# One transformer block on one core: DVE's exponential in two AV products instead of three, and a table of block choices

## The chip, the cores and the metric

The program runs on 1 core of a Trainium2 chip. The metric is device time in microseconds, the median of several executions. The engines named are PE (TensorE matmul; PEld is its weight load), DVE (VectorE), ACT (ScalarE), POOL (GpSimd) and SP (SyncE, which here only issues DMAs).

## The reference

x is 2048 x 512 in bf16, 32 heads of 16, and a gated feed-forward layer with 1,792 inner columns.

```python
def _A_ref(x, wqkv, wo):
    qkv = (x @ wqkv).reshape(B, S, 3, H, Dh)          # H = 32, Dh = 16
    scores = jnp.einsum("bhqd,bhkd->bhqk", q, k) * (Dh ** -0.5)
    p = _softmax(scores, axis=-1)
    o = jnp.einsum("bhqk,bhkd->bhqd", p, v)
    return o.transpose(0, 2, 1, 3).reshape(B, S, D) @ wo
def _B_ref(x, w_gate, w_up, w_down):
    h = _sigmoid(x @ w_gate) * (x @ w_up)
    return h @ w_down
h = x + _A_ref(_layernorm(x), A_wqkv, A_wo)
return h + _B_ref(_layernorm(h), B_w_gate, B_w_up, B_w_down)
```

## The kernel before

**Blocks and tiles.** The scores are 32 heads x 2048 queries x 2048 keys. They are cut into 2,048 blocks of 128 x 512: mostly two tiles of 128 keys by 256 queries side by side. A *group* is four heads by 256 queries (twice as many blocks for the wide groups at the start): 32 blocks. A *tile* `n` is two blocks early on and three later. `scores(n)` (L1085) computes one tile into PSUM; the exponential of a tile is shared out between two engines.

**The two exponentials.** ACT takes all blocks of a tile, or all but the last, in one `activation` (L1408) and writes fp16 into slots of `PT` or of other buffers that have come free (`p_slots`, `more_slots`). If `split` is true, DVE takes the last block: `dexp_first` (L1256) adds an offset to the scores, clips and writes int16. Read as fp16, this *code* is a straight-line approximation of the power of two; two further straight-line pieces, *chords*, are the code plus 326 and the code minus 332. The exponential is approximated by code + first chord + 1.5625 x second chord. In the kernel before these are not added up: all three are fp16 matrices in a tile `J`, and each is multiplied by V on PE, the third by `Vaug2`, which is V times 1.5625. Two DVE blocks share a `J` (`GQ` = 2, six buffers, `QB`). The chords are made by `dexp_rest`: two int64 additions on POOL (L1277), each covering four int16 at once, or, early in the run, on DVE.

**Attention times V.** `av` (L1233) takes blocks whose exponential is ready (a `Unit` each), four at a time in a row, because four heads lie side by side in PE's columns, and adds them up in one PSUM bank `acc`, whose two halves serve alternate groups. `finish_group` lets DVE move a finished group out (L1151), divide by the sums and transpose. `ahead_ready` allows rows of the next group before the present one is finished, within limits that depend on which half it uses.

**Background.** The projections, the output product, the layer norm and the feed-forward layer are generators in a queue `bg`; `try_bg` puts one step of them between the attention's blocks. Their PSUM tiles are moved out by DVE and ACT (tanh, L854). Gate and up weights arrive in `wgu` by DMAs of SP.

**The order.** It is written out by hand (`manual_schedule`): while the program is built, a planner in Python keeps a clock for each engine (`T["P"]`, `T["A"]`, `T["D"]`, `T["G"]`), adds constants for each operation and emits an instruction where its model has the time for it. For every tile the main loop decides about `split`, emits the exponential, and then fills PE's time up to the tile's end with background steps (`try_bg`), rows of AV (`av`), or nothing (`T["P"] += 100`). `want_dve` and the line with `split` limit DVE by its own backlog and by the number of `J` buffers. The result is one fixed instruction stream for each engine. Each stream runs in order, and an instruction that waits holds up all behind it on its engine.

**The end.** After the last tile the remaining AV units are consumed, the last group is finished, and the last 256 queries go through output product, norm and feed-forward; the weights for that are loaded by SP into the `J` buffers (L1495).

Of the kernel before, what the change touches and what calls it, by code (L numbers as in the profile page):

```python
# [19 lines left out]
DependencyClass = mybir.DependencyClass  # L20
DependencyReason = mybir.DependencyReason

LOG2E = 1.4426950408889634
# [119 lines left out]
def kernel(  # L143
# [883 lines left out]
    def pick(want):  # L1027

        out, used = [], set()
        last = None  # L1030
        b = blocks[0]
        if want:
            j = st["dj"] % 4
            if b.a[j]:
                last = (b.qc, b.g, b.a[j].popleft(), j)
                st["dj"] = j + 1
                used.add(j)
        while blocks and len(out) + (last is not None) < wide["n"]:
            b = blocks[0]
            js = [j for j in range(4) if b.a[j]]  # L1040
            if not js:
                blocks.popleft()
                used.clear()
                if last is not None:
                    used.add(last[3])
                continue
            j = max(js, key=lambda j: (j not in used, len(b.a[j]), -((j - st["aj"]) % 4)))
            out.append((b.qc, b.g, b.a[j].popleft(), j))
            st["aj"] = j + 1
            used.add(j)  # L1050
        while blocks and not blocks[0].left():
            blocks.popleft()
        return out + ([last] if last is not None else [])
# [191 lines left out]

    GQ, QB = 2, 6
    quads = []
    half = []

    def dexp_first(src, u, n):  # L1250
        if not half:
            half.append(dvx.tile([P, 3, GQ, QC], I16, name="J", bufs=QB))
            quads.append([])
        J = half[0]
        k = len(half) - 1
        nc.vector.tensor_scalar(out=J[:, 0, k, :], in0=src, scalar1=ZOFF, scalar2=float(-min(CHORDS)),  # L1256
                                op0=ALU.add, op1=ALU.max)
        T["D"] = max(T["D"], sc_end[n] + LAT) + 601
        todo[u[0], u[1], u[3]] += 2
        uns = [Unit(u, J[:, s, k, :].bitcast(FP16), n, None if s else T["D"] + TAIL["D"],  # L1260
                    v=Vaug2 if s == 2 else Vaug) for s in range(3)]
        avq.extend(uns)
        half.append(uns)
        quads[-1].extend(uns)
        if k == GQ - 1:
            dexp_rest()

    def dexp_rest():
        J, quad = half[0], half[1:]
        half.clear()  # L1270
        k = len(quad)

        def words(s):
            return J[:, s, 0:k, :].rearrange("p a b -> p (a b)").bitcast(I64)

        def chord64(s):
            nc.gpsimd.int64_add(words(s), words(0), CHORDS[s - 1] * (1 + 2 ** 16 + 2 ** 32 + 2 ** 48))  # L1277
            for i in range(k):
                quad[i][s].end = T["G"] + TAIL["G"]

        def chord(s):
            nc.vector.tensor_scalar(out=J[:, s, 0:k, :], in0=J[:, 0, 0:k, :], scalar1=float(CHORDS[s - 1]),
                                    scalar2=None, op0=ALU.add)
            for i in range(k):
                quad[i][s].end = T["D"] + TAIL["D"]
        on_pool = len(st["early"]) == TQ * (NQC - 1) and all(j.end is not None for j in st["early"])
        if on_pool and not st["lib"]:
            st["lib"] = True
            T["G"] += 9000.0
        for s in (1, 2):  # L1290
            if on_pool:
                pool(150 + 192 * k, lambda s=s: chord64(s), Mark(T["D"] + TAIL["D"]))
            else:
                chain.append((70 + 133 * k, lambda s=s: chord(s)))

    def want_dve(n):

        quads[:] = [q for q in quads if any(un in avq for un in q)]
        if not blocks or not late("d"):
            return False  # L1300
        busy = sum(j.ns for j in dq if j.ready() is not None) + sum(c[0] for c in chain)
        rest = group_left() / 2.8
        if not half and len(quads) >= QB:
            return False
        if busy > 1500:
            return False
        return busy + 1900 + 1100 * (GQ - len(half[1:])) <= rest * 1100
# [4 lines left out]

    NPT, NPE = 24, 14
    PT = ptp.tile([P, NPT, QC], FP16, name="pt")
# [16 lines left out]
    def run_of(w):  # L1331

        best = None
        for i in range(len(slots) - w + 1):
            row = slots[i:i + w]
            if row[0].tile is row[-1].tile and not any(s.unit in avq for s in row):
                end = max(s.end for s in row)
                if best is None or end < best[0]:
                    best = end, row
# [35 lines left out]
    while n + 1 < len(tiles):  # L1375
# [18 lines left out]
        dable = len(tl) > 1 and busy <= 1500  # L1394
        split = (dable and max(T["D"], sc_end[n] + LAT) <= start + 600 and bool(half or len(quads) < QB))
        if n > N - 12:
            end = max(T["D"], sc_end[n] + LAT) + 1900 + 600 * (GQ - len(half[1:]) if half else GQ)
            split = split and end <= start + 1330 * (N - n) - 500
        if half and half[1][0].u[:2] != tl[-1][:2]:
            dexp_rest()  # L1400
            quads[:] = [q for q in quads if any(un in avq for un in q)]
            split = split and len(quads) < QB
        wa = len(tl) - split
# [19 lines left out]
        hor = max(T["A"], sc_end.get(n + 1, 0.0) + LAT)  # L1423
        lim = ex_end[n] + LAT
        while T["P"] < lim - 100:
            run_dve(min(T["P"], hor))

            def room(mode):
                return lim + OVER - T["P"] - (0 if st["mode"] == mode else SWITCH)
            if early_on or room("dense") >= (bg[0][2][0] if ready_bg(0) is not None else 2 * MM):  # L1430
                used = try_bg(tokens, depth=3 if early_on else 2)
# [44 lines left out]
    nc.vector.tensor_scalar(out=ident2[:], in0=ident_bf[:], scalar1=2.0, scalar2=None, op0=ALU.mult)  # L1476
    while any(un.n < N - 1 and un.slot is not None for un in avq):
        flush()
# [9 lines left out]
    tw = {}  # L1488
    for i in range(QB):
        t = dvx.tile([P, 3, GQ, QC], I16, name="J", bufs=QB)[:].rearrange("p a b n -> p (a b n)")  # L1490
        n = min(3 * GQ // 2, FC - len(tw))
        f = len(tw)
        w = t[:, 0:n * 2 * DC * P].bitcast(BF16).rearrange("p (k c n) -> p k c n", k=2, c=DC)
        for k in range(2):
            nc.sync.dma_start(out=w[:, k], in_=gate_v[k][:, :, f * P:(f + n) * P])  # L1495
        for m in range(n):
            tw[f + m] = w[:, :, :, m * P:(m + 1) * P]
        if len(tw) == FC:
            break

# [35 lines left out]
    leftover(7)  # L1536
    hnl = [PT[:, k, :].bitcast(BF16) for k in range(n)]
    nc.scalar.activation(out=hnl[0], in_=hps[0], func=ACT.Identity, bias=nmr[:, 0:1], scale=rstd[:, 0:1])
# [75 lines left out]
```

## Time and profile before

| | |
|---|---|
| runs | 756.49, 756.53, 757.41 us (median 756.53) |
| profiled execution, span from first to last instruction | 754.6 us |
| granted TensorE clock, mean | 0.998 |
| DVE blocks (L1256) | 619, mean 681 ns |
| ACT exponentials (L1408), all buffers | 695 |
| chord additions on POOL (L1277) | 640, mean 603 ns |
| AV matmuls with `J` (L1233) | 3,546 recorded |
| DMA queue q1 | 39.59 MB, 17.9% of 16 engines' span |

The profile is of one execution, taken by the hardware profiler. A page of it has busy time for each engine, the chain of work that ended last (followed back from the last instruction, at each step to what released it), groups of instructions by line and shape (count, busy time, mean duration, idle time of the engine before them and who ended it), and DMA issues with the time to landing. A timeline row gives the start, the time covered, the engine, the line, what is written and read, and how many instructions are merged in it; in brackets stands the idle time ahead of it and what ended it. On PE and ACT a recorded duration overlaps the start of the next instruction, so that the pace is read from starts, not from durations.

### The profile page before, as it was taken

The numbers are of one execution on the slowest core, as the hardware profiler recorded it, in microseconds if no ns is written. First come the engines' busy times: TensorE is split into PE (matmuls) and PEld (weight loads), VectorE is DVE, ScalarE is ACT, GpSimd is POOL, SyncE is SP. The second block draws the span as 40 slices with busy tenths as digits, with TensorE's granted clock in tenths as the row PEclk, the third lists the DMA queues.
The fourth block names the chain that finished last, engine by engine and source line by source line (L and its number), as shares of the span: only waits on it lengthen the run. The fifth ranks groups of instructions, "written<-read, shape, count | busy, mean of one in ns | idle before, by whom it ended". The sixth has DMA issues, their size and how long they took to land.

```text
span 754.6 us, 27232 instructions
## 1 busy us (share of the span) xinstructions
PE 718.8 (95%) x11541; PEld 347.4 (46%) x11617; DVE 621.7 (82%) x1231; ACT 709.2 (94%) x788; POOL 396.0 (52%) x709
## 2 busy tenths in 40 slices
PE   7999998889999999999999999999999999999997
PEld 3322224444454445444555454535544455445554
DVE  7988878889978898898889688977889777899743
ACT  7989989999999999999999999999999999899952
POOL 2733546666556456655645546564555446465600
PEclk9999999999999999999999999999999999999999
DMA  7000005000123003210222122201321133003160
GB/s 238 1 1 1 1 18 153 2 3 3 30 87 99 10 10 109 78 30 10 78 59 59 36 79 58 74 22 38 99 59 30 44 93 107 10 9 105 47 203 17
DMA packets 68927, 41.65 MB, mean 55 GB/s; under 512 B 3520, under 2 KB 68800, under 8 KB 68800
## 3 DMA queue, kind: packets, MB, share of 16 engines
q1 hardware_dynamic: 68512, 39.59, 17.9%
q8 instruction: 92, 1.51, 0.9%
q14 instruction: 35, 0.29, 0.1%
q10 hardware_dynamic: 288, 0.26, 0.1%
HBM read 37.75 MB, written 2.10 MB: 53 GB/s over the span
## 4 chain that ended last, share of the span: by engine, by line
PE 74%; ACT 13%; DVE 8%; issue 4%; DMA 0%; POOL 0%; DVEq 0%; ACTq 0%; POOLq 0%
PE PS L1085 24%; PE PS L1233 23%; PE PS L824 14%; ACT pt L1408 10%; PE PS L842 6%; DVE J L1256 4%; PE PS L311 2%; PE PS L316 2%; PE PS L763 1%; ACT QTb L1408 1%; DVE xs L1151 1%; ACT xnT L1408 1%; PE PS L1560 1%; DVE st L271 1%; PE PS L305 1%
## 5 line engine op out<-in xcount | busy, mean ns | idle before, releaser
L1277 POOL INT64_ADD J<-J x640 | 377.6, 603 | 305.3 <-DVE J L1256 261.4
L1408 ACT ACTIVATE pt<-PS 128x1024 f16<-128x1024 f32 (+2 forms) x517 | 517.3, 1104 | 13.3 <-PE PS L1085 5.1
L1256 DVE TENSOR_SCALAR J<-PS 128x512 int16<-128x512 f32 x619 | 413.8, 681 | 70.1 <-PE PS L1085 42.7
L1085 PE MATMUL PS<-QT,KT 32*128 32x256 bf16 (+1 forms) x3712 | 263.8, 276 | 10.9 <-ACT pt L1408 4.9
L1233 PE MATMUL PS<-J,Vaug 128*17 128x256 f16 (+1 forms) x3546 | 243.4, 279 | 3.3 <-DVE xs L1151 1.9
L1233 PE MATMUL PS<-pt,Vaug 128*17 128x256 f16 (+1 forms) x2043 | 205.0, 279 | 2.8 <-DVE xs L1151 2.3
L1233 PEld LDWEIGHTS <-Vaug 128*17 128x17 bf16 x6204 | 139.3, 90 | 91.5 <-issue 84.4
L1085 PEld LDWEIGHTS <-KT 32*128 32x128 bf16 x3840 | 89.1, 92 | 197.2 <-issue 193.8
L824 PE MATMUL PS<-xnT,wgu 128*128 128x256 bf16 x784 | 113.7, 275 | 0.1
L1408 ACT ACTIVATE xnT<-PS 128x1024 f16<-128x1024 f32 x90 | 95.0, 1080 | 0.9 <-PE PS L1085 0.7
L824 PEld LDWEIGHTS <-wgu 128*128 128x128 bf16 x784 | 63.6, 97 | 39.6 <-issue 34.2
L1233 PE MATMUL PS<-xnT,Vaug 128*17 128x256 f16 x362 | 56.4, 274 | 0.0
L842 PE MATMUL PS<-wd,hT 128*128 128x512 bf16 x169 | 51.2, 383 | 2.5 <-issue 2.5
L1151 DVE STREAM_TRANSPOSE xs<-PS 128x256 f32<-128x256 f32 (+1 forms) x60 | 27.7, 461 | 21.9 <-PE PS L1233 21.2
L854 ACT ACTIVATE th<-PS 128x512 f32<-128x512 f32 (+1 forms) x63 | 37.4, 594 | 8.4 <-DVE hT L837 6.7
L1408 ACT ACTIVATE QTb<-PS 128x1024 f16<-128x1024 f32 x40 | 42.7, 1068 | 0.5 <-PE PS L1085 0.5
L896 DVE SCALAR_TENSOR_TENSOR hT<-th,PS 128x512 bf16<-128x512 f32 x49 | 33.3, 680 | 7.3 <-PE PS L824 7.2
L1233 PE MATMUL PS<-QTb,Vaug 128*17 128x256 f16 (+1 forms) x158 | 28.4, 275 | 0.0
L1408 ACT ACTIVATE xb<-PS 128x1024 f16<-128x1024 f32 (+2 forms) x26 | 25.6, 1030 | 2.1 <-PE PS L1085 1.1
L1122 DVE TENSOR_TENSOR o<-xs,rsum 128x128 bf16<-128x128 f32 (+1 forms) x60 | 24.4, 407 | 2.1
L1408 ACT ACTIVATE pe<-PS 128x1024 f16<-128x1024 f32 (+2 forms) x22 | 21.7, 1062 | 1.7 <-PE PS L1233 1.4
L842 PEld LDWEIGHTS <-hT 128*128 128x128 bf16 x196 | 12.2, 97 | 20.8 <-issue 17.8
(128 smaller groups left out, 397.5 us busy)
## 6 DMA issues: line engine op xcount, KB each, us to landing
wgu<-in_B_w_gate_dram SPq DMA_DIRECT2D x49, 256.0 KB, 3.0
wgu<-in_B_w_up_dram SPq DMA_DIRECT2D x49, 256.0 KB, 3.5
out_dram<-ob SPq DMA_DIRECT2D x16, 128.0 KB, 2.1
wd<-in_B_w_down_dram SPq DMA_DIRECT2D x1, 1792.0 KB, 8.8
xr<-in_A_x_dram SPq DMA_DIRECT2D x14, 128.0 KB, 3.8
xb<-in_A_x_dram SPq DMA_DIRECT2D x6, 256.0 KB, 6.0
J<-in_B_w_gate_dram SPq DMA_DIRECT2D x4, 384.0 KB, 5.9
J<-in_B_w_up_dram SPq DMA_DIRECT2D x4, 384.0 KB, 7.0
```

What stands on the lines that cost most here:

```text
L311: nc.tensor.matmul(ps, lhsT=w_sb[:, d, p * P:(p + 1) * P], rhs=xnT[c][:, d, :], start=(d == 0), stop=(d == DC - 1))
L824: nc.tensor.matmul(ps[:, 0:PARTS[r][2]], lhsT=w[:, d, :], rhs=hn_of(r)[:, d, :], start=(d == 0), stop=(d == DC - 1))
L842: nc.tensor.matmul(ps, lhsT=hT[:, f, i * P:(i + 1) * P], rhs=wd[:, f, :], start=(f == 0), stop=(f == FC - 1))
L854: nc.scalar.activation(out=th[:, 0:ps.shape[-1]], in_=ps, func=ACT.Tanh, scale=0.5)
L896: nc.vector.scalar_tensor_tensor(out=hT[:, f:f + k, 0:w], in0=th[f][:].rearrange("p (k n) -> p k n", k=k), scalar=1.0, in1=ps2.rearrange(" ...
L1085: nc.tensor.matmul(pss[:, ui, i * CW[qc]:(i + 1) * CW[qc]], lhsT=KT[g // 2][32 * j:32 * j + 32, k * P:(k + 1) * P], rhs=q[32 * j:32 * j + ...
L1122: nc.vector.tensor_tensor(out=o2[:, 0:w // 32, DH * a:DH * a + DH], in0=xs[:, 0:w // 32, 0:DH], in1=rec.to_broadcast([P, w // 32, DH]), op ...
L1151: j = dve(650 - ns[0], lambda: nc.vector.transpose(out=xs[:, 0:w // 32, :].rearrange("p b r -> p (b r)"), in_=src), Mark(T["P"] + DRAIN), ...
L1233: nc.tensor.matmul(dst[32 * j:32 * j + VW, 0:w], lhsT=un.v[:, kt * SPAN[qc] + i, h, :], rhs=un.ap[:, i * w:(i + 1) * w], start=clears and ...
L1256: nc.vector.tensor_scalar(out=J[:, 0, k, :], in0=src, scalar1=ZOFF, scalar2=float(-min(CHORDS)), op0=ALU.add, op1=ALU.max)
L1277: nc.gpsimd.int64_add(words(s), words(0), CHORDS[s - 1] * (1 + 2 ** 16 + 2 ** 32 + 2 ** 48))
L1408: ex = nc.scalar.activation(out=pt, in_=pss[:, 0:wa, :], func=ACT.Exp, scale=AS)
```

## The change

1. A DVE block has two AV units instead of three. Its codes go to a tile `C` of three blocks (`GQ` = 3, `QT_` = 4 buffers). `dexp_rest` takes two runs of slots from the same slots as ACT's exponentials: the first chord is written to the first run, the second to the other. Then a DMA issued on POOL with `accum_op=ALU.add` adds the codes to the first run; it stands in POOL's queue between the two additions. The sum is multiplied by V, the second chord by 1.5625 V. Early in the run, DVE makes both chords and the addition.
2. In the planner the DMA costs POOL 1,100 ns and lands 4,500 ns after that; an int64 addition over k blocks costs 288 + 180 k instead of 150 + 192 k.
3. `room_dve` replaces the count of `J` buffers: it asks for free slots and for the fourth-last `C` to be free by plan. `PT` has 48 slots instead of 24. A run of slots must now be contiguous.
4. A table `PLAN` of 65 entries, with key 16 x tile + step, overrides choices of the planner: 9 ends the filling of a tile, 5 lets PE idle 100 ns, 1 to 3 put in up to so many rows of AV, 4 tries the background first; at step 15 a value forces `split` on (2; five entries) or off, at step 14 it changes which head's block goes to DVE.
5. At the end the weights of the last feed-forward part go into slots of P instead of `J` buffers.

```diff
+PLAN = {96: 9, 162: 4, 304: 3, 305: 4, 322: 3, 417: 4, 432: 1, 624: 3, 638: 1, 640: 2,
...
+        10672: 5, 10702: 2, 10846: 3, 11073: 4, 11087: 2, 11089: 9}
...
-            j = st["dj"] % 4
+            j = (st["dj"] + PLAN.get(16 * len(tiles) + 14, 0)) % 4
...
-    GQ, QB = 2, 6
+    GQ, QT_ = 3, 4
+    DMA_ISSUE, DMA_LAT = 1100.0, 4500.0
...
+    def room_dve():
+        busy = sum(s.unit in avq for s in slots)
+        if len(slots) - busy < 2 * (len(half[1:]) + 1) + 6:
+            return False
+        if half or len(codes) < QT_:
+            return True
+        e = codes[-QT_].end
+        return e is not None and e <= max(T["D"], T["A"]) + 300
...
     def dexp_first(src, u, n):
         if not half:
-            half.append(dvx.tile([P, 3, GQ, QC], I16, name="J", bufs=QB))
-            quads.append([])
+            half.append(dvx.tile([P, GQ, QC], I16, name="C", bufs=QT_))
+            if len(codes) >= QT_:
+                T["D"] = max(T["D"], codes[-QT_].end + LAT)
+            codes.append(Code())
...
-        todo[u[0], u[1], u[3]] += 2
-        uns = [Unit(u, J[:, s, k, :].bitcast(FP16), n, None if s else T["D"] + TAIL["D"],
-                    v=Vaug2 if s == 2 else Vaug) for s in range(3)]
+        todo[u[0], u[1], u[3]] += 1
+        uns = [Unit(u, None, n, None, v=Vaug2 if s else Vaug) for s in range(2)]
...
     def dexp_rest():
...
+        m = T["D"] + TAIL["D"]
+        direct = on_pool and sum(b.left() for b in blocks if (b.qc, b.g) == quad[0][0].u[:2]) < 0
...
+        for s in range(2):
+            at, row = p_slots(k)
+            J.append(row[0].tile[:, row[0].i:row[0].i + k, :])
...
+        def chord64(s):
+            nc.gpsimd.int64_add(words(J[s].bitcast(I16)), words(C[:, 0:k, :]),
+                                CHORDS[s] * (1 + 2 ** 16 + 2 ** 32 + 2 ** 48))
...
+        def add_dma():
+            nc.gpsimd.dma_start(out=J[0], in_=C[:, 0:k, :].bitcast(FP16), accum_op=ALU.add)
+            code.ends[0].end = T["G"] + DMA_LAT
+            for i in range(k):
+                quad[i][0].end = T["G"] + DMA_LAT
...
+        if on_pool:
+            pool(288 + 180 * k, lambda: chord64(0), Mark(max(m, free[0])))
+            if not direct:
+                pool(DMA_ISSUE, add_dma)
+            pool(288 + 180 * k, lambda: chord64(1), Mark(max(m, free[1])))
+        else:
+            chain.append((70 + 133 * k, lambda: chord(1)))
+            chain.append((70 + 133 * k, lambda: chord(0)))
+            chain.append((70 + 264 * k, add_dve))
...
-    NPT, NPE = 24, 14
+    NPT, NPE = 48, 14
...
-        split = (dable and max(T["D"], sc_end[n] + LAT) <= start + 600 and bool(half or len(quads) < QB))
+        split = (dable and max(T["D"], sc_end[n] + LAT) <= start + 600 and room_dve())
+        alt = PLAN.get(16 * n + 15, 0)
+        if alt == 1:
+            split = False
+        elif alt == 2:
+            split = len(tl) > 1 and room_dve()
...
         while T["P"] < lim - 100:
             run_dve(min(T["P"], hor))
+            alt = PLAN.get(16 * n + step, 0)
+            step += 1
...
+            fit = int(room("av") // MM) * 4
+            if alt == 9:
+                break
+            if alt == 5:
+                T["P"] += 100
+                continue
+            if 0 < alt < 4 and fit >= 4 and av(min(4 * alt, fit)):
+                continue
+            if alt == 4:
+                used = try_bg(8.0, depth=2)
...
-    for i in range(QB):
-        t = dvx.tile([P, 3, GQ, QC], I16, name="J", bufs=QB)[:].rearrange("p a b n -> p (a b n)")
+    hrow = take(2)
+    for f in range(0, FC, 2):
+        row = take(4)
```

## The prediction

> **What bounds the kernel now.** I read the page first (shares by engine, then the chain that ended last), then the chain in order of time, then the ACT timeline, the groups with their shapes kept apart, and the DMA issues.
>
> ```profile
> span 754.6 us, 27232 instructions
> PE 718.8 (95%) x11541; PEld 347.4 (46%) x11617; DVE 621.7 (82%) x1231; ACT 709.2 (94%) x788; POOL 396.0 (52%) x709
> PE 74%; ACT 13%; DVE 8%; issue 4%; DMA 0%; POOL 0%; DVEq 0%; ACTq 0%; POOLq 0%
> ```
>
> PE and ACT are both nearly full, and the chain mostly names PE. That invites the reading that PE alone sets the end. The ACT timeline says otherwise:
>
> ```profile
> 289.22 3.88 ACT L1408 ACTIVATE pt<-PS 128x1024 f16<-128x1024 f32 x4
> 292.83 0.75 ACT L854 ACTIVATE th<-PS 128x512 f32<-128x512 f32 x1
> 293.31 4.86 ACT L1408 ACTIVATE pt<-PS 128x1024 f16<-128x1024 f32 x5
> ...
> 639.13 2.39 ACT L1408 ACTIVATE pt<-PS 128x1024 f16<-128x1024 f32 x2
> 644.32 1.45 ACT L1408 ACTIVATE pt<-PS 128x1536 f16<-128x1536 f32 x1 [2.79 <-issue]
> ```
>
> Four exponentials of two blocks start within 292.83-289.22 = 3.61 us, 0.90 us each: back to back. A tanh takes 0.48 us from start to start, and the three-block form 1.33 us (the usual spacing of its starts). Then there are gaps like the one before 644.32, where ACT stands still because the P slots it must write are still held by attention*V (AV) units that have not been consumed.
>
> ```profile
> L1408 ACT ACTIVATE pt<-PS 128x1024 f16<-128x1024 f32 x468 | 455.7, 1075 | 5.3 <-PE PS L1085 3.7 <-PE PS L1233 0.2
> L1256 DVE TENSOR_SCALAR J<-PS 128x512 int16<-128x512 f32 x619 | 413.8, 681 | 70.1 <-PE PS L1085 42.7
> L1233 PE MATMUL PS<-J,Vaug 128*17 128x256 f16 (+1 forms) x3546 | 243.4, 279 | 3.3 <-DVE xs L1151 1.9
> L1277 POOL INT64_ADD J<-J x640: 389/613/825, 41.6 to 717.7; - x160
> ```
>
> Of the 2,048 blocks, DVE approximates 619; ACT does 1,429, as 636 pairs, 49 triples and 10 singles over all buffers that L1408 writes. The exponentials start at 13.1 us and the last one starts at 717.2: 704.0 us. ACT at its own pace needs 636 x 0.903 + 49 x 1.331 + 59 x 0.478 (10 singles, 49 tanh) = 667 us of that. So the loop holds only 37 us in which ACT is not paced by itself: 8 before 100 us, 29 after. This is the first bound on any gain from PE: with the same blocks on ACT, freeing PE entirely brings at most 37 us.
>
> **The change, part by part.**
>
> 1. *One AV product in three goes.* A DVE block now gives two units instead of three. The branch that would keep three (`direct`) needs a sum of queue lengths below zero, so it never runs. Each unit is two matmuls of 256 columns: 619 x 2 = 1,238 fewer. Their price is in the chain:
>
> ```profile
> 326.45 0.77 PE PS L1233 x24
> 352.60 1.43 PE PS L1233 x48
> ```
>
> (1.43-0.77)/24 = 27 ns each, so 1,238 x 27 ns = 33 us of PE. What of it reaches the end is only what ACT waits for. Bounds: 0 (the slots stay scarce) to -35 us (all but the early waits of ACT and a little more). Slots are 24 before and 48 after, but the two products of a DVE block now lie in them too: about 22 slots per group of 32 blocks before, 22 + 2 x 10 = 42 after. 24/22 against 48/42: no more room than before, and a unit now holds its slot through a DMA. I take half of the 29 us: **-15 us**.
>
> 2. *Chords on POOL.* One block takes 389 ns and two take 613 (row above), so 165 + 224 for each block; three take about 837. Blocks are now gathered in threes and a broken three is flushed at each of some 64 groups of 32 blocks; 9.7 blocks per group make 3 to 4 gatherings, about 230 in all. Chords: 2 x (619 x 0.224 + 230 x 0.165) = 353 us, against 378 now. Cost on the path: nothing, as long as POOL keeps up; its cover is what the next part uses.
>
> 3. *230 DMA issues on POOL, each queued between the two chords.* No DMA is issued on POOL in this trace. Lower end: an issue on SP takes 0.37 us; upper end: 2.33 us, the longest of SP's issues near the end. The diff plans 1.1 us, which lies nearer the short rows; I take it, as an estimate. POOL then has 353 + 230 x 1.1 = 606 us of work between 41.6 and 717.7 us (676 us): 90%, against 56% now. That fits, barely. Behind each issue wait the second chord and the next gathering's first; behind those, PE's AV units. At 0.37 us the cost is still nothing; at 2.33 us POOL would have 889 us of work, 213 too many.
>
> ```profile
> 719.20 0.37 SPq L1495 DMA_DIRECT2D J<-in_B_w_gate_dram  x1
> 719.61 2.33 SPq L1495 DMA_DIRECT2D J<-in_B_w_up_dram  x1
> ```
>
> The Trainium skill speaks against this part: "SBUF — State Buffer", section "SBUF: two separate sides", says that descriptors of a DMA issued from POOL cannot be written while DVE runs a two-port operation. By its example (620 ns grow to 3,100 ns) a collision would cost some 2.5 us. The trace's row for the same conflict is mild (INT64_ADD 613 ns median, 825 at most), and DVE's main operations read PSUM. The sum does not use the page.
>
> 4. *Latency.* The DMA moves 384 KB.
>
> ```profile
> wgu<-in_B_w_gate_dram SPq DMA_DIRECT2D x49, 256.0 KB, 3.0
> out_dram<-ob SPq DMA_DIRECT2D x16, 128.0 KB, 2.1
> J<-in_B_w_gate_dram SPq DMA_DIRECT2D x4, 384.0 KB, 5.9
> J<-in_B_w_up_dram SPq DMA_DIRECT2D x4, 384.0 KB, 7.0
> ```
>
> From 128 KB (2.1) to 256 KB (3.0) is 0.9 us, so 384 KB gives 3.9. Low end: queue q1 moved 39.59 MB in 17.9% of the span, 293 GB/s, so 1.3 us over a fixed 1.2: 2.5 us. High end, if the target is read at the same cost: 3.9 + 2.7 = 6.6, close to the 7.0 of two such loads in a row. I take 4.0, below the planned 4.5, with some arriving late beside the weight loads: **+2 us** (0 to +50, see the rivals). "DMA: Bandwidth & Descriptors", section "Anatomy of one DMA — SWDGE (gpsimd) path", would put it at 2.0 us plus bytes at 436 GB/s, 2.9 us, without an addition in it; by it the +2 would be 0. The new traffic is 230 x 384 KB = 90 MB, 41% more DMA share at q1's rate and 82% if it counts twice, beside today's 19%.
>
> 5. *Which blocks DVE gets.* A split saves ACT 0.43 us. The new rule asks for free slots and for the fourth-last code buffer to be free (its DMA landed by plan). One block per group more or less is 64 x 0.43 = 27 us. POOL's 10% of spare work would allow 10 per group (-8), slot shortage could press it to 9.3 (+11). I take no change: **0**.
>
> 6. *The table.* Five of its entries force a split: 5 x 0.43 = **-2 us**; the other 60 move AV rows, idle steps or background blocks and order; a row of four units is 0.22 us, so they are worth -13 to +13, and I take 0.
>
> 7. *The tail.* The last codes go into J at 716.33, and their last AV starts at 721.77:
>
> ```profile
> 716.33 0.65 DVE L1256 TENSOR_SCALAR J<-PS 128x512 int16<-128x512 f32 x1
> 717.15 1.33 POOL L1277 INT64_ADD J<-J  x2 [1.13 <-DVE J L1256]
> 721.77 0.33 PEld L1233 LDWEIGHTS <-Vaug 128*17 128x17 bf16 x8 [0.42 <-issue]
> ```
>
> After: 717.0 + 0.84 + 1.1 + 4.0 to 4.5 = 722.9 to 723.4, 1 to 2 us past that. Bounds 0 (2.5 us latency) to +4: **+2 us**. The weight loads of the last part move from J to freed slots on SP; they still start before the last AV, and PE has the 7 us of leftover down-products as cover.
>
> Sum against the profiled execution: 754.6 - 15 + 2 + 0 - 2 + 2 = 741.6 us of span; its span stands 1.9 us below the median of the runs, 756.53, so **743.5 us**. Part 1 with its bounds and the small terms gives 735 to 752.
>
> **Rivals.**
>
> *A larger gain.* POOL keeps up easily (issue at 0.5 us), splits rise to 10 per group (-8) and the waits of ACT shrink to 8 us (another -6): about 730. For it: POOL was idle 305 us. Against: slots are no more plentiful.
>
> *Hidden anyway.* ACT's own 667 us stay and the slot gaps stay: part 1 becomes 0, the table's 2 us and the tail's 2 cancel: 756, or 754 with a little of part 1. For it: most long gaps of ACT are slot waits, and the latency lengthens them.
>
> *Slower by late DMAs.* The place is PE's in-order queue at the AV of an added unit: everything behind it, the next scores too, waits, and ACT after them. The chain from code to landing is about 0.8 + 1.1 + 4.5 plus 1.5 of gathering, 8 us, so a lateness can be charged 676/8 = 85 times; PE's freed 33 us absorb 0.4 us each time. It decides from a mean latency of 4.9 us; at 5.2 it costs 0.3 x 85 = 25: 768. For it: the 5.9 and 7.0 rows. Against: those load pieces from HBM, several in a row.
>
> *Slower by POOL.* From (676-353)/230 = 1.4 us per issue POOL is full; at 1.5 us its work ends at 41.6 + 353 + 345 = 739.6 instead of 717.7, so 22 us past the old end: 778. For it: POOL is at 90% by plan. Against: the short SP row.
>
> **How the numbers follow.** Forecast (743.5, own range 735 to 752) 0.49; larger gain 0.12; hidden 0.10, half of it faster by a little; late DMAs 0.17; POOL 0.12. About 0.2% (1.5 us) is what a measurement here tells from no change. Faster 0.49 + 0.12 + 0.05 = 0.66, same 0.05, slower 0.29. For the range I leave out the slowest POOL cases and a few ends: 727 to 776.
>
> **What would show it.** Right: about 2,400 matmuls from DVE blocks instead of 3,546; about 230 DMAs on POOL's queue, landing within 4.5 us; ACT's own pace still 0.90 us, its waits after 100 us down from 29 to about 15 us; some 619 codes. Wrong: PE waits at L1233-like AV lines on a DMA, in hundreds of places (late DMAs); POOL with no idle time (POOL); codes far from 619 (part 5); or ACT gaps unchanged with PE idle growing by 33 us (hidden).

## The result and the profile after

The changed kernel takes **799.92 us** (796.25 to 800.72); the kernel before, on the same chip, 756.51 (756.46 to 757.41). The ratio is 1.056 [1.054, 1.058]: slower by 43 us. The prediction was 743.5, with a range of 727 to 776. The profiled execution has a span of 798.3 us against 754.6.

The page of the changed kernel, its span, busy times, DMA queue 0 (the accumulating DMAs) and the clock of PE in 40 slices:

```profile
span 798.3 us, 25394 instructions
PE 734.2 (92%) x10493; PEld 329.7 (41%) x10493; DVE 681.7 (85%) x1253; ACT 707.2 (89%) x788; POOL 596.7 (75%) x786
PEclk9999998799999989999999999999999999999999
q0 software_dynamic: 34416, 83.51, 59.1%
pt<-C POOLq DMA_DIRECT2D x174, 384.0 KB, 4.7
wgu<-in_B_w_gate_dram SPq DMA_DIRECT2D x49, 256.0 KB, 4.6
```

PE has 1,048 recorded matmuls fewer, and yet its busy time rose from 718.8 to 734.2 us; the mean clock fell from 0.998 to 0.970. DVE grew by 60 us, although it makes about as many codes. Queue 0 is new. The gate weights land after 4.6 us at the median, where it was 3.0.

The groups of the page that answer to those shown of before (busy us, mean ns | idle us ahead, and who ended it):

```profile
L1474 ACT ACTIVATE pt<-PS 128x1024 f16<-128x1024 f32 (+1 forms) x568 | 553.6, 1063 | 47.6 <-PE PS L1087 41.0
L1280 DVE TENSOR_SCALAR C<-PS 128x512 int16<-128x512 f32 x640 | 424.1, 679 | 57.1 <-PE PS L1087 40.8
L1235 PE MATMUL PS<-pt,Vaug 128*17 128x256 f16 (+1 forms) x4428 | 217.1, 286 | 19.4 <-DMA pt<-C 13.5
L1325 POOL INT64_ADD pt<-C x429 | 400.1, 1033 | 56.4 <-DVE C L1280 50.3
L1332 POOL DMA_DIRECT2D pt<-C x212 | 185.8, 876 | 66.2 <-POOL pt L1325 53.3
L1124 DVE TENSOR_TENSOR o<-xs,rsum 128x128 bf16<-128x128 f32 (+1 forms) x60 | 51.2, 853 | 2.1
```

Two rows of the page before, to compare with:

```profile
L1408 ACT ACTIVATE pt<-PS 128x1024 f16<-128x1024 f32 (+2 forms) x517 | 517.3, 1104 | 13.3 <-PE PS L1085 5.1
L1122 DVE TENSOR_TENSOR o<-xs,rsum 128x128 bf16<-128x128 f32 (+1 forms) x60 | 24.4, 407 | 2.1
```

Three things are to be seen. ACT now waits 41.0 us for scores; its wait of this kind was 5.1 before. AV waits for a landing (the moment at which a DMA's data are in place). And L1124, which divides a finished group by its sums, takes 853 ns instead of 407.

The table of waits has the rows behind that (engine, line, for whom: us in total, times, longest). Before, PE has no row of waits for codes:

```profile
ACT pt L1474 <- PE PS L1087: 41.0, 62, 4.9
...
PE PS L1087 <- DVE C L1280: 17.4, 24, 1.6
...
PE PS L1235 <- DMA pt<-C: 13.5, 10, 4.6
```

A count of the exponentials tells where the time went. ACT's floor is 0.903 us per pair, 1.331 per triple and 0.478 per single or tanh, the paces of the prediction; the loop reaches from the first exponential's start to the last one's.

| kernel | codes | pairs, triples, singles + tanh | floor | loop | waits of ACT |
|---|---|---|---|---|---|
| before | 619 | 636, 49, 59 | 667.7 | 704.0 | 36 |
| after | 640 | 661, 26, 57 | 658.7 | 744.3 | 86 |

The floor is 9 us lower, the waits are 49 us longer; the loop is 40 us longer. The other 3.4 us of the span's 43.7 lie outside the loop, 3.2 of them behind it (40.6 us from the last exponential's start to the end, 37.4 before).

### The profile page after: what moved, and what is told of

The parts are those of the page before. It is cut to its first block, busy times and chain, and to the rows that moved or that the text cites. A ratio compares the mean times of both kernels' runs of the same rounds, so it can differ in the third digit from the quotient of the medians.

```text
span 798.3 us, 25394 instructions
## 1 busy us (share of the span) xinstructions
PE 734.2 (92%) x10493; PEld 329.7 (41%) x10493; DVE 681.7 (85%) x1253; ACT 707.2 (89%) x788; POOL 596.7 (75%) x786
## 5 line engine op out<-in xcount | busy, mean ns | idle before, releaser
L1474 ACT ACTIVATE pt<-PS 128x1024 f16<-128x1024 f32 (+1 forms) x568 | 553.6, 1063 | 47.6 <-PE PS L1087 41.0
L1280 DVE TENSOR_SCALAR C<-PS 128x512 int16<-128x512 f32 x640 | 424.1, 679 | 57.1 <-PE PS L1087 40.8
L1325 POOL INT64_ADD pt<-C x429 | 400.1, 1033 | 56.4 <-DVE C L1280 50.3
L1087 PE MATMUL PS<-QT,KT 32*128 32x256 bf16 (+1 forms) x3712 | 281.1, 281 | 30.2 <-DVE C L1280 15.9
L1332 POOL DMA_DIRECT2D pt<-C x212 | 185.8, 876 | 66.2 <-POOL pt L1325 53.3
L1235 PE MATMUL PS<-pt,Vaug 128*17 128x256 f16 (+1 forms) x4428 | 217.1, 286 | 19.4 <-DMA pt<-C 13.5
L1235 PEld LDWEIGHTS <-Vaug 128*17 128x17 bf16 x5054 | 112.7, 92 | 101.6 <-issue 86.3
L1474 ACT ACTIVATE xnT<-PS 128x1024 f16<-128x1024 f32 (+1 forms) x58 | 61.1, 1073 | 4.1 <-PE PS L1087 3.7
L1124 DVE TENSOR_TENSOR o<-xs,rsum 128x128 bf16<-128x128 f32 (+1 forms) x60 | 51.2, 853 | 2.1
L1153 DVE STREAM_TRANSPOSE xs<-PS 128x256 f32<-128x256 f32 (+1 forms) x60 | 27.6, 460 | 20.5 <-PE PS L1235 20.0
L1325 POOL INT64_ADD xnT<-C x34 | 30.6, 899 | 2.5 <-ACT QTb L1474 1.1
L326 DVE TENSOR_SCALAR QT<-qd,mask 128x512 bf16<-128x512 bf16 x28 | 24.3, 877 | 0.1
```

What stands on the lines that cost most here:

```text
L1087: nc.tensor.matmul(pss[:, ui, i * CW[qc]:(i + 1) * CW[qc]], lhsT=KT[g // 2][32 * j:32 * j + 32, k * P:(k + 1) * P], rhs=q[32 * j:32 * j + ...
L1124: nc.vector.tensor_tensor(out=o2[:, 0:w // 32, DH * a:DH * a + DH], in0=xs[:, 0:w // 32, 0:DH], in1=rec.to_broadcast([P, w // 32, DH]), op ...
L1153: j = dve(650 - ns[0], lambda: nc.vector.transpose(out=xs[:, 0:w // 32, :].rearrange("p b r -> p (b r)"), in_=src), Mark(T["P"] + DRAIN), ...
L1235: nc.tensor.matmul(dst[32 * j:32 * j + VW, 0:w], lhsT=un.v[:, kt * SPAN[qc] + i, h, :], rhs=un.ap[:, i * w:(i + 1) * w], start=clears and ...
L1280: nc.vector.tensor_scalar(out=C[:, k, :], in0=src, scalar1=ZOFF, scalar2=float(-min(CHORDS)), op0=ALU.add, op1=ALU.max)
L1325: nc.gpsimd.int64_add(words(J[s].bitcast(I16)), words(C[:, 0:k, :]), CHORDS[s] * (1 + 2 ** 16 + 2 ** 32 + 2 ** 48))
```

## Experiments

The medians of before measured beside these runs lie between 756.8 and 757.9 us. Line numbers of a run can be one or two off those of the changed kernel. A *gathering* is one round on POOL: the two additions for up to three codes, and the DMA or what stands in its place.

**Without the DMA**, in the same order, with the table and without it:

```diff
-            nc.gpsimd.dma_start(out=J[0], in_=C[:, 0:k, :].bitcast(FP16), accum_op=ALU.add)
```

> The changed kernel with the adding DMA left out; the order of all other instructions stays as it was, so the code is not added to the first chord (that part of the computation is missing). Theory L (late landings: PE's in-order queue stops at AV units whose DMA has not landed, and its clock falls after each stop): nearly all of the loss goes, 735 to 750 us, and the granted clock is back at 0.99 or more. Theory P (POOL's additions lock DVE out of SBUF, so codes come late): the additions are still there, so 775 us or more, with o<-xs,rsum on DVE still near 870 ns. Theory T (the order made with the table leaves no room for any deviation): between the two, 755 to 775 us.

736.38 us, ratio 0.9715 [0.970, 0.973]. The order with everything in it but the DMA runs 21 us *under* before. So the whole loss, and more, comes with the DMA: 63.5 us.

> The changed kernel with the accumulating DMA left out (the second chord alone is weighed, so the output leaves out the first) and with an empty table. Beside the run without DMA and with the table (736.4). If the table is worth more where nothing disturbs its order than the 6 us that it is worth in the changed kernel: 750 to 756. If it is worth 6 us here too: 742 to 743; then the order with the sum gains about 14 us over before by itself.

749.00 us, ratio 0.9885 [0.987, 0.990]. The result lies between the two expectations: undisturbed, the table is worth 12.6 us and the rest of the order 7.9. By the same count as above: 637 codes, 654 pairs, 31 triples, 59 short ones (singles and tanh), floor 660.03; the loop runs from 13.1 to the end of this row's starts,

```profile
L1473 ACT ACTIVATE pt<-PS x563: 592/1064/1624, 13.1 to 711.9; 128x1024 f16<-128x1024 f32 x179, 128x1536 f16<-128x1536 f32 x7, 128x512 f16<-128x512 f32 x2
```

(durations min/median/max, first and last start). 698.77 - 660.03 = 38.7 us of waits, where before has 36. The fewer matmuls, 33 us by the prediction's price, bought ACT nothing (PE's own busy time fell only from 718.8 to 711.1 us); the gain is that of 18 more codes, 7.7 us of floor. With the table (e1) the waits are 28.6 us: that is what the table is for.

**The table alone taken out of the changed kernel** (`PLAN = {}`):

> The changed kernel with an empty table: every choice is the planner's own. Theories L and P: the losses are made by landings and by the port, whatever the order, so the time moves little, 795 to 815 us (the table's forced splits and moved blocks missing). Theory T: the table gave an order that only its model can run, and without it the loss shrinks: 770 to 790 us.

805.76 us, ratio 1.0634 [1.062, 1.065]. Beside the DMA the table keeps 6 of its 12.6 us, so it isn't what made the kernel slower.

**POOL's time without a DMA.** In place of each DMA POOL writes a 128 x 128 tile that nobody needs, four, five or six times:

```diff
-            nc.gpsimd.dma_start(out=J[0], in_=C[:, 0:k, :].bitcast(FP16), accum_op=ALU.add)
+            for i in range(5):
+                nc.gpsimd.memset(ident2[:], 0.0)
```

> The changed kernel, same order, with six memsets of 128 x 128 bf16 on POOL (about 0.2 us each) in place of each adding DMA (the code is not added to the first chord): POOL is occupied as long as by a DMA's wait and issue, but no DMA is made. e1 (nothing in its place) took 736 us, e5 (an issue of a tiny DMA) 765. Theory A: the issue costs through POOL's time; here too 755 to 768 us. Theory B: it costs because making a DMA's descriptors keeps DVE's two-input operations out of SBUF: 736 to 745 us, with o<-xs,rsum back near 400 to 500 ns.

> As e9 with five memsets in place of each DMA. In e9 six took 1.52 us, so one gathering took POOL some 3.1 us (2.76 planned) and POOL was full: PE waited for its second chords, 792 us. Five take about 1.27 us, 2.9 us a gathering, as long as the wait and the issue of a DMA in the changed kernel and in e5 (2.84), but without descriptors. Theory A (POOL's time): as e5, 755 to 770 us. Theory B (DVE kept out of SBUF by the issue): 736 to 748 us, with o<-xs,rsum at 400 to 500 ns.

> As e11 with four: about 1.02 us, 2.65 us a gathering, just under the plan. Theory A: POOL keeps its plan, 736 to 742 us, and the step from here to e11 is the price of 0.25 us of POOL a gathering. Theory B: 736 to 742 us as well, and e11 no more than 6 us above it.

Four: 735.61 us, 0.9709 [0.969, 0.973]. Five: 740.81, 0.9785 [0.977, 0.980]. Six: 791.7, 1.0449 [1.042, 1.048]. Between five and six there is a cliff. The timeline and the waits of the run with six (start, us; waits as above):

```profile
300.10 1.52 POOL L1333 MEMSET ident<- 128x128 bf16 x6
```

```profile
PE PS L1235 <- POOL pt L1325: 29.2, 47, 2.5
```

At 1.52 us per gathering PE waits for POOL in 47 places: this is what the rival with POOL as the bound looks like. The changed kernel has that wait 4 times, 1.7 us in all. Five memsets give POOL nearly the time that the changed kernel's has: back to back, a gathering takes 2.80 us at the median, 2.84 with the DMA. So POOL's time costs 740.8 - 736.4 = 4 us of the 63.

**The old order with more work on POOL.** The kernel before, its first chord made twice and planned as two:

```diff
-            nc.gpsimd.int64_add(words(s), words(0), CHORDS[s - 1] * (1 + 2 ** 16 + 2 ** 32 + 2 ** 48))
+            for r in range(3 - s):
+                nc.gpsimd.int64_add(words(s), words(0), CHORDS[s - 1] * (1 + 2 ** 16 + 2 ** 32 + 2 ** 48))
...
-                pool(150 + 192 * k, lambda s=s: chord64(s), Mark(T["D"] + TAIL["D"]))
+                pool((3 - s) * (150 + 192 * k), lambda s=s: chord64(s), Mark(T["D"] + TAIL["D"]))
```

> The kernel before, with the first chord's addition on POOL made twice (same result) and planned as two: POOL goes from 378 to about 566 us of additions, no DMA. Theory P: DVE's o<-xs,rsum goes from 390 to 500 ns or more, and the time rises by 8 to 20 us. Theory L: such lengthening does not reach the end, 0 to 5 us.

773.37 us, 1.0212 [1.020, 1.023]. In the old order, with two-block gatherings, 314 more additions on POOL cost 16 us, 14 codes among them (605). The division's mean rose from 390 to 524 ns there, with no DMA on POOL: more additions alone lengthen it too. A busier POOL isn't free in this order, though it was idle 305 us; in the new order it is nearly so.

**The issue without the data.** Every DMA stays on POOL, over 128 rows, but each moves four bytes a row into a spare tile, and no AV waits for it:

```diff
+    nc.gpsimd.memset(ident2[:], 0.0)
...
-            nc.gpsimd.dma_start(out=J[0], in_=C[:, 0:k, :].bitcast(FP16), accum_op=ALU.add)
+            o = 2 * (len(codes) % 64)
+            nc.gpsimd.dma_start(out=ident2[:, o:o + 2].bitcast(FP16), in_=C[:, 0, 0:2].bitcast(FP16), accum_op=ALU.add)
```

> The changed kernel, same order, with each adding DMA issued at the same place on POOL and over the same 128 rows, but moving 2 elements a row between places that nobody waits for (the code is not added to the first chord). It keeps the issue on POOL and takes away the landing wait and the traffic. e1, without any DMA, took 736 us and the changed kernel 800. Theory L (landings): 738 to 750 us. Theory I (the issue: it occupies POOL and locks DVE's two-input operations out of SBUF, o<-xs,rsum 871 ns in the changed kernel, 406 in e1): 770 us or more, with o<-xs,rsum at 700 ns or more.

764.7 us, 1.0085 [1.006, 1.011]. No data to speak of, no landing for AV to wait for, and still 24 us above the five memsets, although these hold POOL longer: the tiny DMA doesn't wait for the addition ahead of it, and a gathering takes 2.23 us at the median instead of 2.80. What differs is DVE. The groups with their shapes kept apart, for the division by the sums: before, without the DMA, with five memsets, with the tiny DMA, after:

```profile
L1122 DVE TENSOR_TENSOR o<-xs,rsum 128x128 bf16<-128x128 f32 x56 | 21.9, 390 | 1.9
```

```profile
L1124 DVE TENSOR_TENSOR o<-xs,rsum 128x128 bf16<-128x128 f32 x56 | 22.8, 407 | 1.9
```

```profile
L1124 DVE TENSOR_TENSOR o<-xs,rsum 128x128 bf16<-128x128 f32 x56 | 23.6, 422 | 1.9
```

```profile
L1125 DVE TENSOR_TENSOR o<-xs,rsum 128x128 bf16<-128x128 f32 x56 | 44.8, 800 | 1.9
```

```profile
L1124 DVE TENSOR_TENSOR o<-xs,rsum 128x128 bf16<-128x128 f32 x56 | 48.8, 871 | 1.9
```

The number behind the comma is the mean in ns. Among these five it doubles where POOL issues DMAs. One such place in the timeline of the changed kernel:

```profile
523.02 0.87 POOL L1332 DMA_DIRECT2D pt<-C  x1 [0.30 <-POOL pt L1325]
...
523.27 2.45 DVE L1124 TENSOR_TENSOR o<-xs,rsum 128x128 bf16<-128x128 f32 x1
...
523.63 1.94 POOL L1325 INT64_ADD pt<-C  x2
...
526.13 1.25 DVE L1280 TENSOR_SCALAR C<-PS 128x512 int16<-128x512 f32 x2
...
526.83 0.37 PE L1087 MATMUL PS<-QT,KT 32*128 32x256 bf16 x2 [1.56 <-DVE C L1280]
```

The division starts 0.25 us into the issue and takes 2.45 us instead of 0.29, until the two additions behind the issue are over too. The next codes, behind it in DVE's queue, are late, and PE's scores wait 1.56 us for the PSUM tile that those codes must empty. Waits of this kind, PE for codes, add up to 0.6 us with five memsets (2 times) and to 12.5 us with the tiny DMA:

```profile
PE PS L1088 <- DVE C L1281: 12.5, 15, 2.0
```

Sorted by what they overlap in the changed kernel: 5 divisions that meet neither an issue nor an addition take 292 ns each, 4 that meet an issue only 292 too, 28 that meet an addition only 619 on average, and 19 that meet an issue and an addition 1,517. With five memsets, 38 that meet additions average 483 ns. An issue by itself is thus not seen to hold the division. Of the 36 divisions over 320 ns in the changed kernel, 34 end 0.13 to 0.20 us after an addition does, and so do all 21 of this length with five memsets: which points to the additions as what holds them. With an issue ahead, the hold begins before the addition's recorded start, and it can last over two additions. Two more of DVE's operations that stay within SBUF grow alike from before to after: QT<-qd from 423 to 877 ns (28 times), hn<-h from 639 to 1,184 (14 times). The three make 47 us of DVE. Its codes, which read PSUM, take 681 and 679 ns, unchanged.

The Trainium skill has a rule that bears on it: "SBUF — State Buffer", section "Who interferes with whom", says that a DVE instruction with two SBUF inputs contends with a POOL instruction that reads SBUF, not with one that only writes it, and that the later one is blocked for the whole of the other. That five memsets leave the division at 422 ns agrees, and so do the ends of the held divisions, right behind those of additions, which read SBUF. The page's warning on DMAs issued from POOL tells of the other direction, DVE keeping the descriptors back; the 2.45 us above is a division of DVE's, held by POOL.

**The whole transfer, but no AV waits for it.** The full-sized accumulating DMA goes to scratch memory in HBM, and AV reads the first chord without the codes added:

```diff
+    scr = [nc.dram_tensor(f"scr{i}", (128, GQ, QC), FP16, kind="Internal").ap() for i in range(8)]
...
-            nc.gpsimd.dma_start(out=J[0], in_=C[:, 0:k, :].bitcast(FP16), accum_op=ALU.add)
+            nc.gpsimd.dma_start(out=scr[len(codes) % 8][:, 0:k, :], in_=C[:, 0:k, :].bitcast(FP16), accum_op=ALU.add)
```

> The changed kernel, same order, with the full-size adding DMA going to eight scratch areas in HBM in turn: issue and traffic of the same kind, but no AV unit waits for it (the code is not added to the first chord; DVE still waits until a code buffer has been read). Theory L: 740 to 755 us, a little above e5. Theory I: as e5, 770 us or more. If e5 is fast and this one is slow, the traffic is to blame.

771.07 us (to 780.07), 1.0223 [1.016, 1.029]: 6 us above the tiny DMA. DVE does still wait here, 9.6 us in 16 places, for a `C` that a DMA has not read yet (3.9 us in 9 places in the changed kernel). The remaining 29 us to 799.92 are the wait for the landing, together with what else differs between a target in HBM and one in SBUF, which wasn't told apart. The interval is wide: the border between the two terms is known to some 5 us.

The same wait was to be taken out in another way, with the DMA kept as it is: AV reads the second chord twice, in place of the sum and itself.

```diff
-                un.ap = J[s][:, i, :]
+            for i in range(k):
+                quad[i][s].ap = J[s][:, i, :]
+                quad[i][0].ap = J[s][:, i, :]
```

> The changed kernel with all its DMAs, but the AV unit that should read the sum reads the second chord instead, so PE waits for no landing (the sum is made and not used; one product is thus of other data). POOL issues and DMA traffic are unchanged. Theory L: about as e1, 740 to 755 us. Theory P: 780 to 800 us, because POOL's issues and additions are all there; o<-xs,rsum on DVE near 870 ns. If e1 is fast and this is slow, the issues on POOL are to blame rather than the landings.

871.67 us, 1.1503 [1.148, 1.152], slower than all others, and by a fault of the edit: the second chord's slot counts as free once its own unit is consumed, so it can be refilled while the other unit still has to read it; PE waits up to 4.6 us for additions (18 times) and up to 7.8 us for DMAs (4 times). It says nothing on the landing.

**Planning for a later landing** (`DMA_LAT` 6,500 instead of 4,500, no table):

> The changed kernel with an empty table (e3, 806 us) and the DMA planned to land 6,500 ns after its issue instead of 4,500. Theory L: planned waits replace the unplanned stops and the drops of the clock, 770 to 790 us. Theory I: DVE's delays stay and the longer latency is paid on top, 810 us or more.

802.01 us, 1.0589 [1.055, 1.063]: 3.8 under the same kernel planned with 4.5 us. AV's waits for landings do shrink (16.2 us in 14 places to 6.9 in 3, for slots of `pt`), and ACT's by the count above from 88 to 69 us; but only 604 codes are made instead of 637, which costs 14 us of floor. The lateness isn't cured by a more careful constant; that slots are then held longer fits the missing codes.

**Three units again, with the rest of the change** (`direct` always true, no table: no sum, no DMA):

> The changed kernel with an empty table and the branch 'direct' always taken: three AV units per DVE block as before, no DMA; what stays of the change is gathering in threes, chords written to P slots and 48 slots. Both theories: no DMA, so no such losses; PE has its 33 us again: 758 to 768 us. If it were 775 us or more, something else of the change costs as well.

765.54 us, 1.0118 [1.010, 1.014]. By the exponentials' count 589 codes only, so the floor is 680.6. Against e14 (749.0), which has two units for each block, a third one costs 16.5 us: 20.5 of floor, less 5.9 of waits (32.8 against 38.7), and 2 that lie outside the profiled spans (which differ by 14.6). The third unit reads the codes in `C`, so that `C` is free only when AV has read it; that fits the 48 codes fewer. Two units are worth having here because more codes are made with them, not because ACT waits less.

**The down weights in 14 pieces.** In the changed kernel one 1,792 KB load falls into the worst stretch. The timelines of PE and ACT there, of DVE and PE a little later, and the windows (us; busy and count of PE, PEld, DVE, ACT, POOL; clock; DMA share; GB/s):

```profile
119.75 0.40 PE L1087 MATMUL PS<-QT,KT 32*128 32x256 bf16 x6
124.80 1.01 PE L1235 MATMUL PS<-pt,Vaug 128*17 128x512 f16 x3 [4.64 <-DMA pt<-C]
```

```profile
126.40 2.17 ACT L1474 ACTIVATE pt<-PS 128x1024 f16<-128x1024 f32 x2 [4.86 <-PE PS L1087]
```

```profile
140.25 2.23 DVE L1124 TENSOR_TENSOR o<-xs,rsum 128x128 bf16<-128x128 f32 x1
...
143.13 0.49 PE L1087 MATMUL PS<-QT,KT 32*128 32x256 bf16 x2 [1.13 <-DVE C L1280]
```

```profile
120.00:130.00 10.00, 5.36 (x70) 1.85 (x66) 4.02 (x8) 4.09 (x5) 5.17 (x7) 0.66 1.09 266
130.00:160.00 30.00, 27.11 (x403) 9.68 (x399) 22.71 (x36) 26.43 (x28) 23.36 (x31) 0.83 0.69 132
```

Three accumulating DMAs landed after 9.2, 8.9 and 8.2 us here. PE stands still for 4.64 us and the clock is at half from 122.8 us for 6.8 us, which makes the mean of 0.66: a late landing is paid a second time by a slower PE. The 0.83 behind it has another origin. It is one stretch at half clock, 10.2 us from 143.3 on, and right ahead of it PE waits 1.13 us for codes that a division held for 2.23 us has delayed. Of the ten stretches at half clock in the changed kernel, nine begin within 3 us of a wait of PE of 1.13 us or more: four for landings (17 us at half clock), five for DVE behind a division or an hn<-h of over 1.7 us (27 us). The tenth lies at the very end. So the held operations of DVE, too, are paid twice.

```diff
+        if fw is not None and wd_left and n % 4 == 0:
+            f0 = wd_left.pop(0)
+            nc.sync.dma_start(out=wd[:, f0, :], in_=wd_v[:, f0, :])
...
-            nc.sync.dma_start(out=wd[:], in_=B_w_down.rearrange("(f p) n -> p f n", p=P))
+            wd_v = B_w_down.rearrange("(f p) n -> p f n", p=P)
+            wd_left = list(range(FC))
```

> The changed kernel, whole, with the 1,792 KB load of wd cut into 14 pieces, one every fourth tile. In the changed kernel three adding DMAs issued beside that load take 8 to 9 us, PE stops 4.6 us for one of them, and its clock is halved for 17 us soon after. Theory L (late landings): the stop goes and most of that slow stretch, 786 to 794 us. If the time stays within 3 us of 800, a single long stop is made up elsewhere.

793.98 us, 1.0468 [1.042, 1.051], 6 under the changed kernel. SP issued the pieces only about 1 us apart, so the load was hardly spread; the same three landings took 8.4, 8.0 and 7.6 us, PE still stood for 3.89 us, and both stretches at half clock are still there. The question is left open by this run.

**A table without the DMA.** The kernel before with the change's hooks for a table, and 45 entries made for its own order by its own planned durations:

```diff
+PLAN = {96: 9, 976: 5, 1150: 1, 1216: 3, 1504: 5, 1536: 1, 1632: 9, 1728: 9, 1744: 9, 1905: 1,
...
+            alt = PLAN.get(16 * n + step, 0)
+            step += 1
```

> The kernel before, with the change's way of reading a table (the same codes at the same places) and a table of 45 entries that was made for this order, with no sum of two chords and no accumulating DMA. By the durations with which the order is written the table takes 7 us out of it. If such an order holds on the chip wherever nothing new lies in it: about 749 us (747 to 752), ratio about 0.990. If a table's gain is lost to durations that the order doesn't know, as most of the change's seems to be: 756 +-2.

749.85 us (749.54 to 750.0), ratio **0.990 [0.989, 0.992]**: faster than both kernels, and within 1 us of what was expected. Its page:

```profile
span 747.8 us, 27266 instructions
PE 723.2 (97%) x11594; PEld 346.7 (46%) x11594; DVE 622.0 (83%) x1228; ACT 709.3 (95%) x788; POOL 394.1 (53%) x711
```

ACT's floor is 669.0 us here (633 pairs, 52 triples, 59 short ones), its loop 698.6, its waits 30 us instead of 36.

## Why the prediction was wrong

The runs form a row in which each adds one thing. Each is the median of its own run, and the medians of before beside them differ by 1 us, so the small steps are good to some 2 us:

| step | us | change | the prediction's term |
|---|---|---|---|
| before | 756.9 | | |
| order with the sum, no DMA, no table (e14) | 749.0 | -8 | parts 1 and 5: -15 and 0 |
| with the table (e1) | 736.4 | -13 | part 6: -2 |
| POOL's time for the issue, as memsets (e11) | 740.8 | +4 | parts 2 and 3: 0 |
| a real issue, no data (e5) | 764.7 | +24 | part 3: 0 |
| all the data, AV doesn't wait (e6) | 771.1 | +6 | part 4: +2, with the next |
| AV waits for the landing (after) | 799.9 | +29 | part 4: +2 |

**The step that failed is part 3 with part 4: the accumulating DMA was priced at 0 and +2 us, and it costs 63.5.**

About half of the loss is PE's own slower work. From five memsets to the tiny DMA the span grows by 27.0 us, of which PE's busy time makes 15.2 (704.0 to 719.2), with 30.7 us at half clock instead of 7.1. From e6 to the changed kernel it grows by 29.7, of which PE's busy time makes 14.7 (719.5 to 734.2), with 49.5 us at half clock instead of 20.7. The prediction has no term for the clock.

*Part 3.* The 1.1 us taken for an issue was good: 0.30 us of wait and 0.87 of issue. POOL kept up, as forecast, and the rival with POOL as the bound was wrong for this kernel, though its price was sound: it put the point of decision at 1.4 us per issue, and the cliff of the memsets lies between five, 1.25 us in the timeline, and six, 1.52 us. What failed is "That fits, barely", by which an issue of 1.1 us stands in the sum with nothing. The part asked who waits for POOL, and nobody asked whom POOL's issue keeps waiting on another engine. It even quoted a conflict between DVE and the descriptors and set it aside because the chords' durations were mild; that row shows POOL's side with no DMA in the trace, and the loss is on DVE's side. That the 24 us come from the stretched DVE operations follows from the pair e5 and e11 and from the rows that differ between them: the three operations take 29 us more, PE's waits for codes go from 0.6 to 12.5 us, and all six of these waits of over 0.9 us come right behind a DVE operation of 1.9 to 2.9 us. No run took the conflict away while it kept the DMA, so this much is inferred; and why an issue makes the hold longer than the additions alone do is open.

*Part 4.* The latency itself was near: from the issue's start, the median is 4.6 and the mean 4.73, against a price of 4.0, an upper end of 6.6, and a plan of 4.5 behind the issue's 1.1. By the mean, the rival of late DMAs wasn't even to begin: it was to decide from 4.9 us. But the order isn't late by the mean. 40 of 239 landings came more than 5.6 us after the issue's start (the planned 1.1 and 4.5), the longest after 9.2:

```profile
DMA to landing us min/median/max: 2.6/4.6/9.2
```

With a gate or up load in flight the median is 5.1 us, without 4.0. Ten times a late one stops PE's queue, the scores behind it and so ACT; that is the rival's own place, though not the hundreds of waits that the prediction named as its sign. Its price of 25 us is near the 29 measured, but by luck: it is a lateness of 0.3 us paid 85 times, and the trace has 13.5 us in ten waits and 14.7 us more of PE's busy time. Its 768 is too low because it has nothing for the issue. The clock was at half for 49.5 us of the changed kernel, 5.1 of before. By the fit in the Trainium skill, "DMA: Bandwidth & Descriptors", section "Anatomy of one DMA — SWDGE (gpsimd) path", such a transfer is estimated at 2.9 us, as the prediction noted; the shortest here took 2.6 and the median 4.6.

*Part 1* doubted that PE's freed 33 us reach ACT otherwise than through slots, and still took half of 29 us. In e14 ACT waits 38.7 us, before 36: nothing of the 15 arrived. That slots were what ACT waited for before was argued, not shown: the row that was read so names no releaser ([2.79 <-issue]), and the profile puts only 4 us of ACT's waits there down to AV. The range of 735 to 752 isn't what part 1's bounds give either; 0 and -35 in the sum make 723.5 and 758.5. And "hidden anyway" leaves out the +2 of part 4. The sentence "no more room than before" was in the working; the value that followed from it was the low bound, 0. *Part 5* chose 0 inside -8 to +11: 18 to 21 more codes were made, worth 8 to 9 us, the end at which POOL keeps up. *Part 6* chose -2 inside -15 to +11; it is -13 undisturbed and -6 beside the DMA. So the gain side, -17 in the prediction, is -20.5 on the chip, nearly right in sum, by luck, from other terms than named. *Part 7*, the tail, +2: 3.2 us were added behind the loop.

Of the rivals, "hidden anyway" had the right reason for part 1, "slower by late DMAs" for nearly half of the loss.

## What to carry to other kernels

Price a DMA issued from POOL three times: on POOL's queue, on DVE's operations within SBUF that run beside it and the POOL work behind it, and at its consumer by the slow tail of its landings rather than the mean. Where PE waits over a microsecond, look at the granted clock behind the wait as well. In an order written out by hand, a latency with a spread of several us is a different thing from a long fixed duration, and here a later planned landing moved the cost into fewer codes. Time freed on an engine is worth nothing until it is shown what wait of the engine that matters it ends; here 33 us of matmuls ended none.

## What was not expected of the hardware

- Where POOL issues DMAs between additions, DVE's operations within SBUF are held longer than beside additions alone: the division of 291 ns took up to 2,449 ns in the changed kernel and up to 2,908 with the tiny DMA, and at most 949 ns with five memsets in the DMA's place, where its mean was 422 ns.
- The additions' records grow as well, but not their pace. An addition over three blocks is recorded with 825 ns alone and with some 1,140 behind an issue, and with the tiny DMA the additions to P average 1,058 ns, with five memsets 770 (below). But such a record starts 0.27 us before the issue's own ends, and from the issue's end to the end of two three-block additions it is 1.67 us in the changed kernel, from the memsets' end 1.61:

```profile
L1326 POOL INT64_ADD pt<-C x429 | 428.0, 1058 | 101.1 <-DVE C L1281 80.5 <-ACT pt L1476 5.8 <-DVE nw L292 4.8
```

```profile
L1325 POOL INT64_ADD pt<-C x429 | 326.0, 770 | 16.3 <-DVE C L1280 15.2 <-DVE mv L276 0.8
```

- In the changed kernel, half clock for 3.4 to 10.2 us came behind single waits of PE as short as 1.13 us, though not behind each: one of 1.16 us at 248.1 us was followed by none. Without a DMA (e1) there is a stretch of 10.2 us behind waits of no more than 0.52 us, so the length of one wait doesn't decide it.
- 83.5 MB of SBUF-to-SBUF additions took 59% of the DMA engines' span, where 39.6 MB of loads take 17%, and lengthened the landing of the gate weights from 3.0 to 4.6 us; with the tiny DMA it stayed at 3.0.
